# Output projection of a recurrent-memory attention kernel: partial sums per column tile, 256 columns wide, folded by a stacked identity

## The chip, the cores and the metric

The kernel runs on one core of a Trainium2 chip. A core has a matrix engine (TensorE, in the profile PE, with its weight loads as PEld), a vector engine (DVE), a scalar engine (ACT), GpSimd (POOL), and queues that start DMA transfers (here all on SP). The engines run their own instruction streams in order and wait for one another by semaphores. Matrix products are written to PSUM, eight banks of 512 float32 values in each of 128 partitions, and are read from there by ACT or DVE; PE reads its operands from SBUF. The metric is device time in microseconds of one execution, the median of the runs.

## The reference

One sequence of 2048 tokens with 512 features goes through two attentions, A and B, which a gate per token mixes. A walks through 64 segments of 32 tokens. Each segment has 8 memory rows in front, and the first 8 rows of its output are the next segment's memory: that makes the segments a chain.

```python
for s in range(n_seg):                      # 64 segments of 32 tokens
    h = jnp.concatenate([mem, xs], axis=1)  # 8 + 32 rows, 512 features
    q = jnp.einsum('btd,dhe->bhte', h, Wq)  # 32 heads of 128
    k = jnp.einsum('btd,dhe->bhte', h, Wk)
    v = jnp.einsum('btd,dhe->bhte', h, Wv)
    scores = jnp.einsum('bhqe,bhke->bhqk', q, k) * scale
    p = _softmax(jnp.where(mask, scores, -1e9))
    o = jnp.einsum('bhqk,bhke->bhqe', p, v)
    o = jnp.einsum('bhte,hed->btd', o, Wo)  # sums over 32 heads and 128 channels
    mem = o[:, :M, :]                       # the next segment's memory, M = 8
    outs.append(o[:, M:, :])
...
return g * a + (1 - g) * b                  # b: attention B, causal in 4 blocks of 512, 32 heads of 16
```

The line that the change rewrites is the product with Wo.

## The kernel before

The program is written out in full. Python code makes lists of operations for each engine (`Prog`), and `emit` turns every dependency on another engine into a semaphore wait. What stands first in an engine's list runs first.

A prologue transposes x, makes B's projections and loads the weights; it ends at a barrier some 96 us into the span. Then `plan_a` writes the 64 segments. Of the 40 rows of a segment, the 8 memory rows and the first 24 tokens make up 32 rows in `hT` (features on partitions); these are in the recurrence. The last 8 tokens of each of four segments are put together as 32 "left" rows, so their Q, K and V (`left_units`) and their product with Wo (`ol_units`) are done once per group of four. These products are fillers ("Fc") at two places in a segment: in the first three of a group six Q, K and V passes of the next group's left rows, and in the last the two halves of the former group's Wo product (`ol`).

The order within a segment is written by hand in `A_ORDER` (L823). Q0 to V1 are passes over half of the heads, 16 matmuls of 512 columns each. S, M, N are scores, softmax sums and normalisation of a half; PV is the product with V into four PSUM banks, E its copies to SBUF (`OT_sb`). W0 and W1 are the Wo product of heads 0 to 15 and 16 to 31. WT brings its result into `hT` for the next segment. The other names are fillers: bS scores a tile of B (two banks, then an exponential of 1024 columns on ACT and one or two masks on POOL), bP multiplies the oldest such tile with V, and bT does one step that waits in B's `late` list: `chain` (one small product, then three DVE steps, or seven and a sum on POOL for jobs past the first block) or `finish` (a transpose on PE, a copy on DVE, a store). bS is let through while fewer than two tiles are scored and not yet multiplied, and while the count stays on a line of 160 tiles over 57 segments. Ff makes output rows: a Wo product for B, a transpose of A's rows, the mixing.

Wo before (`out_rows`, L893): the stationary operand of a matmul is one head's 32 output rows, 128 x 32, which fills a quarter of the array's columns. Four matmuls, j = 0 to 3, take the same head four times and put a quarter of Wo's 512 columns (32-column blocks j, j+4, ...) into PSUM partitions 32j to 32j+31. All 32 heads add up in one bank of 128 columns. ACT copies it to `aW_sb` (`aO_sb` for the left rows), and a DVE transpose of 32 x 32 blocks (`flip`) turns it into `hT`'s form. POOL copies the 24 token rows to `aT_st`, where A's rows are collected for the output.

PSUM banks are handed out by `Banks`: `take` one, `pair` two neighbours, `give` back as soon as the reading operation is planned; who takes a bank next waits for that reader.

Of the kernel before, what the change touches and what calls it, by code (L numbers as in the profile page):

```python
# [223 lines left out]
def build(nc, es, A_x, A_mem0, A_Wq, A_Wk, A_Wv, A_Wo, B_wq, B_wk, B_wv, B_wo, B_beta, gate_w, out, dbg=None):  # L224
# [31 lines left out]
    def alloc(stack, *specs):  # L256
        for name, shape, dt, n in specs:
# [3 lines left out]
    alloc(es, ("ident", [128, 128], BF16, 0), ("xT", [128, C, S], BF16, 0), ("hT", [128, C, 128], BF16, 2),  # L261
# [9 lines left out]
          ("aTg", [128, C, 128], BF16, 0))  # L271
# [13 lines left out]
          ("OT_sb", [128, H, L], BF16, 0), ("OTL", [128, H, SEG], BF16, 2), ("aW_sb", [128, 128], BF16, 0), ("aO_sb", [128, 128], BF16, 0),  # L285
# [16 lines left out]
    def Rs(name):  # L302
        if name not in R:
            R[name] = Res(name)
            if name.startswith(("P0", "P1", "Pn", "R0", "R1", "OT", "aW", "aO", "t1", "aTx", "aTl")):
                R[name].readers = list(v.stores)
        return R[name]
# [60 lines left out]
def plan_const(v):  # L368
# [28 lines left out]
    def late():  # L397
        rob, rmk = Rs("onesb"), Rs("mneg")
        gp(lambda g: g.memset(onesb[:], 0.0), rob, "onesb0", True)
        gp(lambda g: g.memset(mneg[:], 0.0), rmk, "mneg0", True)  # L400
        for j in range(4):
            q = slice(32 * j, 32 * j + 32)
            gp(lambda g, q=q: g.memset(onesb[q, q], 1.0), rob, "onesb1_%d" % j)
            for i in range(4):
                o = (L + 16) * i
                sel(mneg[q, :, o + M:o + L], [[0, 4], [1, 32]], ALU.is_ge, NEG, M, -1, rmk, "mneg1_%d" % j)
                sel(mneg[q, :, o + L:o + L + 16], [[-8, 4], [0, 16]], ALU.is_ge, NEG, 0, 1, rmk, "mneg2_%d" % j)
                sel(mneg[q, :, o + L:o + L + 16], [[8, 4], [0, 16]], ALU.is_ge, NEG, 7, -1, rmk, "mneg3_%d" % j)
                sel(mneg[q, :, o + L + 8:o + L + 16], [[8, 4], [1, 8]], ALU.is_ge, NEG, 0, -1, rmk, "mneg4_%d" % j)
# [228 lines left out]
class BAttn:  # L638
# [185 lines left out]
    Q1 K0 Q0 K1 V0 TK0 TQ0 S0 bP bP TQ1 TK1 bS V1 M0 S1 N0 Fc M1 PV0 E0a N1 E0b Fc PV1 E1b E1a W0 W1 WT bS bT Ff Ff Ff  # L824
    bS bP bS""".split()
# [4 lines left out]
def plan_a(v, nseg):  # L830
# [10 lines left out]
    OT_sb, OTL, aW_sb, aO_sb, t1_sb, aT_st, g_sb, omg_sb, out2d, g_out = (  # L841
        v.OT_sb, v.OTL, v.aW_sb, v.aO_sb, v.t1_sb, v.aT_st, v.g_sb, v.omg_sb, v.out2d, v.g_out)
# [50 lines left out]
    def out_rows(bk, b, lhs, reads, name):  # L893

        def f(pe):
            ins = None
            for h in range(16 * b, 16 * (b + 1)):
                for j in range(4):
                    ins = pe.matmul(pb[bk][SEG * j:SEG * (j + 1), 0:128], lhs(h), cols(Wo_sb[:, h, :], j), start=(h == 0), stop=(h == H - 1))  # L899
            return ins  # L900
        P.op("pe", f, reads=reads + [Rs("Wo")], writes=[rbank[bk]], name=name)

    def ol_units(g):
# [5 lines left out]
        for b in range(2):  # L909
            def u(b=b):  # L910
                if b == 0:
                    st["bk"] = B.take(long=True)
                bk = st["bk"]
                out_rows(bk, b, lambda h: OTL[par][:, h, :], [Rs("OTL%d" % par)], "ol%d_%d" % (g, b))
                if b == 1:
                    evac(ENG["OL"], aO_sb[:, :], pb[bk][:, 0:128], [bk], [Rs("aO")], "olev%d" % g)
                    B.give(bk)
            units.append(("c", u))

        def ut():  # L920
            flip(aT_st[par][:, :, :].rearrange("p c (r t) -> p c r t", t=SEG)[:, :, :, SEG - 8:SEG],
                 aO_sb[:, :].rearrange("p (c r i) -> p c r i", c=C, i=8), [Rs("aO")], [Rs("aTl%d" % par)], "aTl%d" % g)
            stored.append(g)
            if g == ngrp - 1:
                return
            P.dma(P.group("as%d" % g, "as%d" % par), lambda sp: sp.dma_start(v.aTd[g], aT_st[par][:, :, :]),
                  reads=[Rs("aTl%d" % par)] + [Rs("aTx%d_%d" % (par, r)) for r in range(4)], writes=[Rs("aTd%d" % g)], name="sta%d" % g)
# [50 lines left out]
    def segment(s, fill):  # L978
# [109 lines left out]
        def wo(b):  # L1088

            if b == 0:  # L1090
                wb["bk"] = B.take()
            bk = wb["bk"]
            out_rows(bk, b, lambda h: OT_sb[:, h, 0:SEG], [Rs("OT%d_%d" % (b, half)) for half in range(2)], "wo%d_%d" % (s, b))
            if b == 1:
                evac(ENG["W"], aW_sb[:, :], pb[bk][:, 0:128], [bk], [Rs("aW")], "wev%d" % s)
                B.give(bk)

        def w_t():

            nxt = (s + 1) % 2  # L1100
            rm = Rs("hTm%d" % nxt)
            quads = hT[nxt][:, :, :].rearrange("p c (k z) -> p c k z", z=SEG)
            flip(quads[:, :, :, 0:M], aW_sb[:, :].rearrange("p (c k t) -> p c k t", c=C, t=M), [Rs("aW")], [rm], "hm%d" % (s + 1))
            P.op("gp", lambda gq: gq.tensor_copy(
                aT_st[par][:, :, SEG * r:SEG * (r + 1) - M].rearrange("p c (k t) -> p c k t", t=M), quads[:, :, 1:4, 0:M]),
                 reads=[rm], writes=[Rs("aTx%d_%d" % (par, r))], name="atx%d" % s)
# [117 lines left out]
```

The softmax here doesn't subtract the row's maximum and nothing guards it: scores larger than these inputs give would overflow.

## Time and profile before

| | |
|---|---|
| median of 3 runs | 1060.99 us (1060.31 to 1063.03) |
| span of the profiled execution | 1059.6 us |
| mean granted TensorE clock | 0.962 |
| Wo of the segments (L899, OT_sb) | 8192 matmuls, 151.8 us busy |
| Wo of the left rows (L899, OTL) | 2048 matmuls, 37.0 us busy |
| copy to aW_sb, ACT | 64 x 278 ns |
| transpose to hT, DVE | 64 x 312 ns |
| copy of rows to aT_st, POOL | 64 x 269 ns |

The profile is of one execution. In a group's line stand the line of the code, the engine, the operation, what it writes and reads, the shape and the count; then busy time, the mean duration in ns, and the engine's idle time just before these instructions with what ended it ("issue": nothing that the profile shows). A busy time is the union of the durations: four matmuls on four column tiles run side by side, so a mean duration is not a rate. In the timeline each line has the start, the duration, the engine and line, and the count of merged instructions, with the idle time before it in brackets.

### The profile page before, as it was taken

The page shows a single profiled execution, that of the slowest core. Times are in us where ns is not written, and L with a number is a line of the kernel's source. Part 1 is how long each engine was busy: PE and PEld are TensorE (multiplying, and loading weights), DVE is VectorE, ACT ScalarE, POOL GpSimd, SP SyncE. Part 2 cuts the span into 40 slices and gives each one's busy share as a digit, 9 for nine tenths or more (in the row PEclk, how much of TensorE's full clock was granted, in tenths as well). Part 3 has the DMA queues.
Part 4 walks back from the last instruction along what each step waited for, and adds up shares of the span by engine and source line. Part 5 has one row for each costly group of instructions (what it writes and reads, how often), then busy time and mean ns, then how long its engine had stood idle before and what let it go on. Part 6 is the DMA issues. An engine that isn't in the chain of part 4 may idle for free.

```text
span 1059.6 us, 65320 instructions
## 1 busy us (share of the span) xinstructions
PE 923.4 (87%) x30149; PEld 565.4 (53%) x30149; DVE 558.8 (53%) x1198; ACT 586.0 (55%) x1211; POOL 229.2 (22%) x603
## 2 busy tenths in 40 slices
PE   7967999898988989889898999899898889988886
PEld 4434555555555545555555565555555555555544
DVE  4655555453554636465465646565464546446433
ACT  4442666565665655656565656665565666544444
POOL 6100222221222122222221222222222212211010
PEclk9998999999999989999899999999899999989999
DMA  8897000000101110000001101000111001000110
GB/s 287 265 323 256 12 13 16 17 17 12 25 14 41 38 34 20 24 15 20 20 20 44 39 22 34 14 25 15 24 40 35 22 19 39 10 14 4 40 33 9
DMA packets 65929, 52.23 MB, mean 49 GB/s; under 512 B 34288, under 2 KB 64120, under 8 KB 64120
## 3 DMA queue, kind: packets, MB, share of 16 engines
q1 hardware_dynamic: 65656, 48.06, 15.5%
q8 instruction: 236, 3.87, 1.5%
q14 instruction: 37, 0.30, 0.1%
HBM read 33.47 MB, written 14.57 MB: 45 GB/s over the span
## 4 chain that ended last, share of the span: by engine, by line
PE 72%; issue 9%; ACT 8%; DVE 6%; DMA 3%; SPq 1%; ACTq 0%; POOL 0%; DVEq 0%
PE ps L862 33%; PE ps L899 17%; PE ps L706 5%; ACT PT L714 4%; PE ps L753 4%; PE ps L582 2%; DVE LN_sb L321 2%; PE ps L1061 2%; PE ps L557 2%; ACT R_sb L1043 2%; PE ps L949 2%; ACT R_sb L1040 2%; DVE Pn_sb L1047 2%; DMA scr_pQd<-stgp 1%; DMA Wo_sb<-in_A_Wo_dram 1%
## 5 line engine op out<-in xcount | busy, mean ns | idle before, releaser
L899 PE MATMUL ps<-Wo_sb,OT_sb 128*32 128x128 bf16 x8192 | 151.8, 229 | 52.5 <-issue 51.3
L714 ACT ACTIVATE PT<-ps 128x1024 bf16<-128x1024 f32 x160 | 160.5, 1023 | 26.2 <-PE ps L706 21.9
L899 PEld LDWEIGHTS ps<-Wo_sb,OT_sb 128*32 128x32 bf16 x8192 | 127.4, 101 | 67.1 <-issue 59.2
L722 POOL TENSOR_SCALAR_AFFINE_SELECT PT<-PT 128x256 bf16<-128x256 bf16 (+1 forms) x224 | 98.8, 441 | 277.0 <-ACT PT L714 269.1
L862 PE MATMUL ps<-Wq_sb,hT 128*32 128x512 bf16 x2048 | 143.9, 396 | 2.8 <-DVE hT L868 1.9
L862 PE MATMUL ps<-Wk_sb,hT 128*32 128x512 bf16 x2048 | 139.0, 387 | 0.0
L319 ACT ACTIVATE KN_sb<-ps 128x512 bf16<-128x512 f32 x128 | 76.4, 597 | 108.6 <-PE ps L862 105.8
L868 DVE STREAM_TRANSPOSE hT<-aW_sb 128x128 bf16<-128x128 bf16 x64 | 19.9, 312 | 219.9 <-ACT aW_sb L319 219.9
L862 PE MATMUL ps<-Wv_sb,hT 128*32 128x512 bf16 x2048 | 134.9, 381 | 0.8 <-ACT V_sb L319 0.8
L319 ACT ACTIVATE OT_sb<-ps 128x320 bf16<-128x320 f32 x256 | 96.9, 430 | 55.4 <-PE ps L1070 54.4
L868 DVE STREAM_TRANSPOSE KT_sb<-KN_sb 128x512 bf16<-128x512 bf16 x128 | 88.4, 690 | 48.9 <-ACT KN_sb L319 48.6
L319 ACT ACTIVATE aW_sb<-ps 128x128 bf16<-128x128 f32 x64 | 17.8, 278 | 149.3 <-PE ps L899 146.1
L868 DVE STREAM_TRANSPOSE QT_sb<-QN_sb 128x512 bf16<-128x512 bf16 x128 | 83.5, 690 | 11.7 <-ACT QN_sb L319 10.6
L1129 POOL COPY OTL<-OT_sb 128x256 bf16<-128x256 bf16 x64 | 25.5, 398 | 295.5 <-ACT OT_sb L319 295.5
L862 PEld LDWEIGHTS ps<-Wk_sb,hT 128*32 128x32 bf16 x2048 | 57.3, 99 | 59.1 <-issue 5.7
L862 PEld LDWEIGHTS ps<-Wq_sb,hT 128*32 128x32 bf16 x2048 | 51.9, 99 | 63.3 <-issue 16.6
L321 DVE CAST V_sb<-ps 128x512 bf16<-128x512 f32 x64 | 44.3, 692 | 74.9 <-PE ps L862 74.9
L862 PEld LDWEIGHTS ps<-Wv_sb,hT 128*32 128x32 bf16 x2048 | 50.4, 96 | 54.4 <-ACT P_sb L1019 9.8
L321 DVE CAST QN_sb<-ps 128x512 bf16<-128x512 f32 x64 | 44.0, 687 | 41.4 <-PE ps L862 41.3
L706 PE MATMUL ps<-QTj,KTj 32*128 32x384 bf16 (+3 forms) x512 | 64.2, 309 | 0.0
L1040 ACT ACTIVATE R_sb<-ps 128x160 f32<-128x160 f32 x128 | 38.9, 304 | 36.6 <-PE ps L1036 36.3
L1047 DVE TENSOR_TENSOR Pn_sb<-P_sb,R_sb 128x160 bf16<-128x160 bf16 x128 | 42.6, 333 | 30.9 <-ACT R_sb L1043 21.9
(117 smaller groups left out, 1424.1 us busy)
## 6 DMA issues: line engine op xcount, KB each, us to landing
Wk_sb<-in_A_Wk_dram SPq DMA_DIRECT2D x4, 1024.0 KB, 7.0
Wq_sb<-in_A_Wq_dram SPq DMA_DIRECT2D x4, 1024.0 KB, 8.6
Wv_sb<-in_A_Wv_dram SPq DMA_DIRECT2D x4, 1024.0 KB, 8.4
Wo_sb<-in_A_Wo_dram SPq DMA_DIRECT2D x4, 1024.0 KB, 10.0
scr_vd<-V SPq DMA_DIRECT2D x16, 136.0 KB, 5.3
Vj<-scr_vd SPq DMA_DIRECT2D x32, 68.0 KB, 2.4
Wo_sb<-in_A_x_dram SPq DMA_DIRECT2D x4, 512.0 KB, 7.4
scr_kTd<-stgk SPq DMA_DIRECT2D x16, 128.0 KB, 6.5
```

What stands on the lines that cost most here:

```text
L319: P.op("act", lambda a: a.activation(dst, src, ACT.Copy), reads=[v.rbank[k] for k in bks], writes=dres, name=name)
L321: P.op("dve", lambda d: d.tensor_copy(dst, src), reads=[v.rbank[k] for k in bks], writes=dres, name=name)
L706: ins = pe.matmul(v.pb[bks[x]][:, o:o + w], KT[e][r, 128 * kc:128 * (kc + 1)], QT[r, q0:q0 + w], start=True, stop=True, tile_position=(r.s ...
L714: P.op("act", lambda a: a.activation(pt[:, :, :], v.ps[:, bks[0]:bks[1] + 1, :], ACT.Exp, scale=v.SCALE_B), reads=[v.rbank[b] for b in bks ...
L722: P.op("gp", lambda g, mv=mv: g.affine_select(mv, mv, [[0, mv.shape[1]], [1, 128]], ALU.is_ge, 0.0, base=0, channel_multiplier=-1), reads= ...
L753: ins = pe.matmul(v.pb[ob][:, o:o + 17], pt[:, x, col:col + 128], V[:, kc, 17 * h:17 * (h + 1)], start=first, stop=True, skip_group_check= ...
L862: ins = pe.matmul(pb[bk][SEG * j:SEG * (j + 1), :], lhs(c), cols(w, j) if split else w[:, 512 * j:512 * (j + 1)], start=(c == 0), stop=(c ...
L868: P.op("dve", lambda d: d.transpose(dst, src), reads=reads, writes=writes, name=name)
L899: ins = pe.matmul(pb[bk][SEG * j:SEG * (j + 1), 0:128], lhs(h), cols(Wo_sb[:, h, :], j), start=(h == 0), stop=(h == H - 1))
L1040: P.op("act", lambda a: a.activation(R_sb[:, b, :], pb[bk][:, 224:384], ACT.Ln), reads=[rbank[bk]], writes=[Rs("R%d" % b)], name="ln%d_%d" ...
L1047: P.op("dve", lambda d: d.tensor_tensor(wide(Pn_sb, b)[:, :, 0:L], wide(P_sb, b)[:, :, 0:L], R_sb[:, b, :].rearrange("p (i q) -> p i q", q ...
L1129: P.op("gp", lambda gq: gq.tensor_copy(OTL[par][:, :, 8 * r:8 * r + 8], OT_sb[:, :, SEG:L]), reads=[Rs("OT%d_%d" % (c, hf)) for c in range ...
```

## The change

Four matmuls now take four different heads, 4k to 4k+3, each in its own column tile, and multiply 256 columns of Wo at once; a second set of matmuls does the other 256 columns into a second bank. After 8 steps of k, partition 32j + t of the two banks holds row t summed over the heads that are j modulo 4. These four partial sums still have to be added across partitions. `part_ev` copies each bank to bf16 on ACT (the high part) and subtracts that from the bank on DVE, which gives the rest, again in bf16 (the low part). `fold` multiplies both parts as stationary operands (128 x 128) with a stacked identity (`fold`, 128 x 32: four identities of 32 one above the other) and so adds the four partial sums and transposes the result in one go: 8 matmuls of 32 columns into one bank. DVE copies 8 columns per block of features to `hT`, ACT the other 24 to `aT_st`.

The left rows go the same way. They use `LN_sb` for the two parts, and their last unit (`ut`), a DVE transpose before, is now a fold and an ACT copy.

The order at the end of a segment changes: after W1 come bS, bT and bP, then WT, which is PE work now, then bS, Ff three times, bP and bS. `hT` is 32 columns wide instead of 128, and the stacked identity is made on POOL in the prologue.

```diff
-    Q1 K0 Q0 K1 V0 TK0 TQ0 S0 bP bP TQ1 TK1 bS V1 M0 S1 N0 Fc M1 PV0 E0a N1 E0b Fc PV1 E1b E1a W0 W1 WT bS bT Ff Ff Ff
-    bS bP bS""".split()
+    Q1 K0 Q0 K1 V0 TK0 TQ0 S0 bP bP TQ1 TK1 bS V1 M0 S1 N0 Fc M1 PV0 E0a N1 E0b Fc PV1 E1b E1a W0 W1 bS bT bP WT bS Ff Ff Ff
+    bP bS""".split()
...
+        rf = Rs("fold")
+        gp(lambda g: g.memset(v.fold[:], 0.0), rf, "fold0", True)
+        for j in range(4):
+            sel(v.fold[:], [[-1, SEG]], ALU.not_equal, 1.0, -SEG * j, 1, rf, "fold1_%d" % j)
...
-    def out_rows(bk, b, lhs, reads, name):
...
-            for h in range(16 * b, 16 * (b + 1)):
-                for j in range(4):
-                    ins = pe.matmul(pb[bk][SEG * j:SEG * (j + 1), 0:128], lhs(h), cols(Wo_sb[:, h, :], j), start=(h == 0), stop=(h == H - 1))
...
+    HD = 128 * C // 2
...
+    def out_part(bks, b, lhs, reads, name):
+
+        for hf in range(2):
+            def f(pe, hf=hf):
+                ins = None
+                for k in range(4 * b, 4 * b + 4):
+                    for j in range(4):
+                        ins = pe.matmul(pb[bks[hf]][SEG * j:SEG * (j + 1), 0:HD], lhs(4 * k + j), Wo_sb[:, 4 * k + j, HD * hf:HD * (hf + 1)],
+                                        start=(k == 0), stop=(k == 7))
+                return ins
...
+    def part_ev(bks, hi, lo, res, name):
+
+        for hf in range(2):
+            c = slice(HD * hf, HD * (hf + 1))
+            src = pb[bks[hf]][:, 0:HD]
+            P.op("act", lambda a, c=c, src=src: a.activation(hi[:, c], src, ACT.Copy), reads=[rbank[bks[hf]]],
...
+            P.op("dve", lambda d, c=c, src=src: d.tensor_tensor(lo[:, c], src, hi[:, c], ALU.subtract),
...
+    def fold(bk, hi, lo, res, name):
+
+        for hf in range(2):
+            def f(pe, hf=hf):
+                ins = None
+                for c in (2 * hf, 2 * hf + 1):
+                    for n, t in enumerate((hi, lo)):
+                        ins = pe.matmul(pb[bk][:, SEG * c:SEG * (c + 1)], t[:, 128 * c:128 * (c + 1)], v.fold[:, :], start=(n == 0), stop=(n == 1))
...
-                    st["bk"] = B.take(long=True)
...
+                    st["bks"] = B.pair()
+                out_part(st["bks"], b, lambda h: OTL[par][:, h, :], [Rs("OTL%d" % par)], "ol%d_%d" % (g, b))
                 if b == 1:
...
+                    part_ev(st["bks"], LN_sb[:, 0, :], LN_sb[:, 1, :], o_res, "olev%d" % g)
+                    B.give(*st["bks"])
...
         def w_t():
 
             nxt = (s + 1) % 2
-            rm = Rs("hTm%d" % nxt)
-            quads = hT[nxt][:, :, :].rearrange("p c (k z) -> p c k z", z=SEG)
-            flip(quads[:, :, :, 0:M], aW_sb[:, :].rearrange("p (c k t) -> p c k t", c=C, t=M), [Rs("aW")], [rm], "hm%d" % (s + 1))
-            P.op("gp", lambda gq: gq.tensor_copy(
-                aT_st[par][:, :, SEG * r:SEG * (r + 1) - M].rearrange("p c (k t) -> p c k t", t=M), quads[:, :, 1:4, 0:M]),
-                 reads=[rm], writes=[Rs("aTx%d_%d" % (par, r))], name="atx%d" % s)
+            bk = B.take()
+            src = fold(bk, v.WH, v.WL, w_res, "wf%d" % s)
+            evac("dve", hT[nxt][:, :, 0:M], src[:, :, 0:M], [bk], [Rs("hTm%d" % nxt)], "hm%d" % (s + 1))
+            evac(ENG["W"], aT_st[par][:, :, SEG * r:SEG * (r + 1) - M], src[:, :, M:SEG], [bk], [Rs("aTx%d_%d" % (par, r))], "atx%d" % s)
+            B.give(bk)
```

## The prediction

> **What bounds the kernel now.** I read the page first (busy shares, chain, groups), then the groups by form, then the timeline of single segments. One column of times runs through all: TensorE (PE) is the engine that sets the end.
>
> ```profile
> PE 923.4 (87%) x30149; PEld 565.4 (53%) x30149; DVE 558.8 (53%) x1198; ACT 586.0 (55%) x1211; POOL 229.2 (22%) x603
> ...
> PE 72%; issue 9%; ACT 8%; DVE 6%; DMA 3%; SPq 1%; ACTq 0%; POOL 0%; DVEq 0%
> ```
>
> ACT and DVE are half idle, so work added to them costs only where PE waits for it. The second line is the chain that ended last: "issue", 9%, is PE waiting for nothing visible. The groups by form say where (last columns: idle before, and what ended it):
>
> ```profile
> q8 instruction: 236, 3.87, 1.5%
> ...
> L899 PE MATMUL ps<-Wo_sb,OT_sb 128*32 128x128 bf16 x8192 | 151.8, 229 | 52.5 <-issue 51.3 <-DMA Wo_sb<-in_A_Wo_dram 1.1
> L899 PE MATMUL ps<-Wo_sb,OTL 128*32 128x128 bf16 x2048 | 37.0, 220 | 13.8 <-issue 13.8
> L1061 PE MATMUL ps<-Pn_sb,V_sb 32*128 32x40 bf16 x2048 | 36.5, 178 | 12.4 <-issue 8.4 <-DVE Pn_sb L1051 3.7
> L1070 PE MATMUL ps<-Pn_sb,VL 32*128 32x16 bf16 x2048 | 33.7, 165 | 5.7 <-issue 5.7
> ```
>
> The queue line explains it: 236 packets of 3.87 MB are 16.4 KB each, and 2 x 30149 PE instructions (a weight load and a matmul each) over 236 are 255. So PE's instructions arrive in blocks of 256. In a dense stretch the stalls sit one block apart:
>
> ```profile
> 742.56 0.52 PE L899 MATMUL ps<-Wo_sb,OTL 128*32 128x128 bf16 x24 [0.80 <-issue]
> ...
> 746.16 0.27 PE L1061 MATMUL ps<-Pn_sb,V_sb 32*128 32x40 bf16 x16 [1.68 <-issue]
> ...
> 749.91 1.04 PE L899 MATMUL ps<-Wo_sb,OT_sb 128*32 128x128 bf16 x32 [1.61 <-issue]
> ```
>
> 3.60 and 3.75 us lie between restarts with 128 matmuls (256 instructions) in each: a block is supplied in about 3.7 us, and PE stalls wherever it eats one faster. The Wo matmuls eat one in 2.
>
> The end of an undisturbed segment (start, duration), what the change rebuilds:
>
> ```profile
> 550.17 2.11 PE L899 MATMUL ps<-Wo_sb,OT_sb 128*32 128x128 bf16 x128
> ...
> 552.22 0.39 PE L706 MATMUL ps<-QTj,KTj 32*128 32x512 bf16 x2
> 552.39 0.28 ACT L319 ACTIVATE aW_sb<-ps 128x128 bf16<-128x128 f32 x1 [1.24 <-PE ps L899]
> ...
> 552.71 0.31 DVE L868 STREAM_TRANSPOSE hT<-aW_sb 128x128 bf16<-128x128 bf16 x1 [2.01 <-ACT aW_sb L319]
> 552.71 1.02 ACT L714 ACTIVATE PT<-ps 128x1024 bf16<-128x1024 f32 x1
> ...
> 553.80 0.41 POOL L722 TENSOR_SCALAR_AFFINE_SELECT PT<-PT 128x256 bf16<-128x256 bf16 x1 [0.45 <-ACT PT L714]
> ```
>
> Call T the start of the last Wo matmul (here 552.07). The carried memory is in hT at T+0.95 and the next Q pass could start at T+1.0; B's scores and PV fill that time, so the recurrence is hidden. A score tile is exponentiated (1.02) and masked (0.41) 2 us after its matmul.
>
> [...] below, 16 matmuls of 512 columns take 0.86 to 0.88 us, so 0.216 a group of four. For 256 columns I estimate 0.109 from it. [...] adot, 256 elements, 0.42 us.
>
> **The change, part by part.**
>
> *Fewer PE instructions.* Per segment 128 Wo matmuls become 64; per group of four segments the left rows' (ol) 128 become 64; each gains 8 fold matmuls. 64 x 64 + 16 x 64 - 80 x 8 = 4480 pairs less of 30149, 201 blocks for 236. Stalls now: the rows above give 51 + 14 + 8 + 6 = 79 us of issue, 82 with small rows. Idle counts from a modelled end 0.17 after the next start would have been (229 - 56 ns), so some 84 stalls hide 14 more: 96 us. After: from S1 to the end of Wo a plain segment has 72 + 32 + 16 + 64 + 32 + 64 + 128 = 408 instructions in about 5.2 us, where it had 536 in 5.3. Its densest 256 take about 2.9 us, 0.8 under the supply, the 256 before about 3.4. A stall is then 0 to 1.1 us by where the block's edge falls; I take 0.25 a segment, 16 us. Gain 80 (bounds 48, half the stalls staying, and 96).
>
> *The Wo matmuls themselves.* 16 groups of 0.109 for 32 of 0.056, but W1's first matmul waits for the last OT copy, 1.03 us after W0 began, before and after (ACT is no faster). From there 0.76 for 0.85: gain 0.09 x 64 = 6.
>
> *The chain to hT.* ACT copies of 256: between 278 (128), 430 (320) and 597 ns (512), so 0.38. First half's banks are ready 0.43 earlier. Against T: high parts end at 0.33 and 0.75, low parts (0.42 each on DVE) at 0.78 and 1.21; fold can run at 0.83 and 1.26. PE has bS and bP (0.31 + 0.25) and reaches it at about 0.8, so it waits some 0.3, then 0.14 of matmuls. The PSUM copy to hT (0.17) follows: Q possible at 1.8. Not the last wait, though.
>
> *The moved bP.* With the new order the final bP of a segment takes the tile that the bS just after W1 scored. (Before, that tile was taken in the next segment, 6 us later.) Its exp now starts after two copies, at 0.77, ends 1.79; POOL's mask is one of 0.41, two of 0.44, or one of 0.64, and the bP can start at 2.3, 2.8 or 2.5. PE is there at 1.7. Everything behind it in PE's queue, first the next Q pass, waits: Q starts at 2.6 to 3.05, mean 2.8, where it started at 1.1. One bP of 0.25 is gone from the next segment's front. Loss per plain segment 2.8 - 1.1 - 0.25, with the variants 1.38.
>
> *The chain on DVE.* bT is now ahead of the fold, so its DVE steps are ahead of the copy to hT:
>
> ```profile
> 539.86 0.22 DVE L786 RECIPROCAL rden<-ps 128x16 f32<-128x16 f32 x1
> ...
> 540.20 1.05 PE L862 MATMUL ps<-Wq_sb,hT 128*32 128x512 bf16 x16
> ...
> 541.08 1.04 PE L862 MATMUL ps<-Wk_sb,hT 128*32 128x512 bf16 x16
> ...
> 541.67 0.43 DVE L802 TENSOR_TENSOR amem<-ps,rden 128x256 f32<-128x256 f32 x1
> ...
> 541.94 1.04 PE L862 MATMUL ps<-Wq_sb,hT 128*32 128x512 bf16 x16
> ```
>
> 2.15 us from the first to the free engine. In the 24 segments with such a chain (jobs with sb above 0) hT is ready at 1.13 + 2.15 + 0.17, Q at 3.5: loss 2.1. With output rows (Ff: t1 0.87, transposes 0.22) PE is covered longer and was late before: 1.1 with a chain, 0.6 without.
>
> Counting slots by the code's rules (at most two tiles pending, 160 tiles over 57 segments): 32 x 1.38 + 14 x 2.1 + 10 x 1.1 + 2 x 0.6 = 86; the last six segments, without B tiles, lose 0.8 to 1.5: 7. Together 93 (bounds 70, if PE comes later to the bP than I count, and 110).
>
> *The left rows.* They hold a pair of banks over PV0, so PV0's second pair is now one whose Ln (L1040) must be read first: +0.47. OT's copies then queue on ACT behind the two new copies, and W0 waits for the low parts in the pair it takes over. Against shorter ol matmuls +0.5 net, in 15 segments: 7 (bounds 0 and 13). Waits that the old stalls hid (OT copies, Pn) appear: 5.
>
> *At nothing:* five GpSimd instructions for the stacked identity, where POOL has 70 us until A starts; smaller hT; the dropped POOL copy (POOL 22% busy) and its replacement on ACT, behind the exp, which nobody waits for early. No DMA is added; SP keeps its order.
>
> Sum: 93 + 7 + 5 - 80 - 6 = +19. The clean lengths that I set against stalled segments already leave out about 8 us of other waits at the segment ends (bP waiting for POOL and DMA, about 4 us in the rows; half-clock stretches), which the new wait would cover: +11. On the span, 1059.6 + 11 = 1070.6; the runs' median lies 1.4 above the span, so about 1072; I say 1071.
>
> **Rivals.** *Fetch relief wins (faster).* If almost no stall remains (gain 96) and the late bP's wait overlaps more (loss 76), 76 + 7 + 5 - 96 - 6 - 8 = -22: 1039. [...] It decides once the segment ends lose under 1.25 us on average instead of 1.45. Against it: the 2.3 to 2.8 is durations in series on three engines. *The stalls stay.* If PV and scores, still 7 ns a matmul, inherit half of them (gain 48): +43, 1104. For it: L1061 and L1070 show issue stalls now; against: these were mostly tails of runs begun by ol. *It cancels*: both large terms are within 12 us of each other, so 1058 to 1064 is no accident. *The change not doing what it says*: nothing speaks for it; the counts are fixed by the loops.
>
> **How the numbers follow.** No change is within 0.3%, about what a measurement of this kernel can tell. Forecast (1064 to 1090) 0.48; stalls stay 0.16; both slower. Fetch relief wins 0.26. Cancels 0.10. The range 1046 to 1095 takes in the cancelling case and the near halves of the outer two and leaves out a fifth; the forecast's own is 1064 to 1090.
>
> **What would show it.** PE issue idle falls from 82 to under 20; if not, the second rival. The bP matmuls (L753 before) wait for POOL's mask by some 40 us in total, Q for hT by 20 or more; if both are small, the first. Fold waits for DVE about 0.3 us each. Wo matmuls take half the count at about 275 ns. A wait of PV0 for ACT's Ln in ol segments only. It is wrong if segment ends (last Wo to Q) are under 2.2 us in the mean.

## The result, and the profile after

The changed kernel takes 1074.41 us (median of 4 runs, 1071.62 to 1077.59), the kernel before 1060.65 (4 runs beside it, 1058.26 to 1063.03). The ratio is 1.0125, with a 95% interval of 1.0081 to 1.0169: slower by a bit over one per cent. A ratio leaves out executions more than 1.5% above the fastest of the same kernel, so it can differ a little from the quotient of two medians. The profiled execution has a span of 1071.9 us, where it was 1059.6, and a mean clock of 0.968.

The page of the changed kernel, the lines that answer to those of before (busy shares, the queue that carries instructions, the chain that ended last):

```profile
PE 945.5 (88%) x25647; PEld 564.9 (53%) x25669; DVE 610.0 (57%) x1342; ACT 638.0 (60%) x1371; POOL 212.0 (20%) x544
...
q8 instruction: 202, 3.31, 1.3%
...
PE 3%; ACT 1%; DVE 1%; issue 0%; ACTq 0%
```

PE runs 4480 pairs of weight load and matmul less (the weight loads went from 30149 to 25669; the trace lacks 22 records of matmuls), and 202 instruction packets come for 236: 2 x 25669 instructions over 202 are 254 a packet, where it was 255. The chain was followed back over the last segments only (its shares add up to 5% of the span), so it can't be set against the one of before; "issue" is gone from what it shows. The groups by form say the same for the whole run (last columns: idle before, and what ended it):

```profile
L867 PE MATMUL ps<-Wq_sb,hT 128*32 128x512 bf16 x2048 | 142.3, 400 | 8.2 <-DVE hT L322 7.9
L909 PE MATMUL ps<-Wo_sb,OT_sb 128*32 128x256 bf16 x4096 | 140.6, 286 | 17.2 <-DVE LN_sb L921 9.2 <-DVE VL L322 3.0 <-DMA Wo_sb<-in_A_Wo_dram 2.3
...
L758 PE MATMUL ps<-Vj,PT 128*128 128x17 bf16 x1280 | 57.4, 172 | 26.0 <-POOL PT L727 25.3 <-issue 0.2
...
L1096 PE MATMUL ps<-Pn_sb,V_sb 32*128 32x40 bf16 x2048 | 35.9, 178 | 12.3 <-ACT R_sb L1075 6.1 <-DVE Pn_sb L1086 3.7 <-issue 1.8
...
L909 PE MATMUL ps<-Wo_sb,OTL 128*32 128x256 bf16 x1024 | 34.0, 274 | 0.2 <-issue 0.2
...
L931 PE MATMUL ps<-fold,WH 128*128 128x32 bf16 x256 | 29.2, 177 | 13.6 <-DVE WL L921 12.1
```

The Wo matmuls hardly wait for anything invisible any more (51.3 and 13.8 us before). In their place stand waits with a name: bP (L758) for POOL's mask 25.3 us, the fold (L931) for the low parts 12.1, the Q pass for hT 7.9, PV (L1096) for ACT's Ln 6.1.

Two numbers taken over all segments from the trace hold the balance. A segment's Wo matmuls, from the first start to the last, took 2.96 us in the mean and take 1.97: 63 x 0.99 = 62 us gained. From the start of the last Wo matmul to the first Q matmul of the next segment went 1.52 us in the mean and go 2.95: 63 x 1.43 = 90 us lost. The span grew by 12.3, so all the rest gained 16 by difference. One bP less at the front of 57 segments is 14 of that, by the prediction's estimate of 0.25 us each. That leaves 2 us for everything else, so what the left rows and the PV rows gained in stalls must about have been given back, to new waits such as the 9.2 us (W0 for the low parts of the left rows) and 6.1 us (Ln) in the rows above.

A segment end in the timeline (start, duration), one in which the chain of B's memory is due:

```profile
542.00 1.93 PE L909 MATMUL ps<-Wo_sb,OT_sb 128*32 128x256 bf16 x64 [0.43 <-DVE LN_sb L322]
...
543.55 0.82 ACT L919 ACTIVATE WH<-ps 128x256 bf16<-128x256 f32 x2 [1.07 <-PE ps L909]
...
543.96 0.86 DVE L921 TENSOR_TENSOR WL<-ps,WH 128x256 bf16<-128x256 f32 x2 [1.27 <-PE ps L909]
...
544.36 1.02 ACT L719 ACTIVATE PT<-ps 128x1024 bf16<-128x1024 f32 x1
...
544.74 0.25 DVE L791 RECIPROCAL rden<-ps 128x16 f32<-128x16 f32 x1
...
544.97 0.18 PE L931 MATMUL ps<-fold,WH 128*128 128x32 bf16 x1 [0.18 <-DVE WL L921]
...
545.45 0.88 POOL L727 TENSOR_SCALAR_AFFINE_SELECT PT<-PT 128x256 bf16<-128x256 bf16 x2 [2.52 <-ACT PT L719]
...
546.39 0.37 PE L758 MATMUL ps<-Vj,PT 128*128 128x17 bf16 x8 [0.84 <-POOL PT L727]
546.39 0.42 DVE L807 TENSOR_TENSOR amem<-ps,rden 128x256 f32<-128x256 f32 x1
...
546.74 0.18 DVE L322 CAST hT<-ps 128x32 bf16<-128x32 f32 x1
...
547.06 1.90 PE L867 MATMUL ps<-Wq_sb,hT 128*32 128x512 bf16 x16 [0.30 <-DVE hT L322]
```

The sum of the fold has been in PSUM since about 545.2. Its copy to hT starts only at 546.74, behind the chain on DVE (L791 to L807, 544.74 to 546.81). PE meanwhile stands at a bP, for a mask whose exponential began behind the two new copies on ACT. Two late things end close together, and the Q pass pays for the later one. The last line shows a third thing: this Q pass took 1.90 us, where one takes 1.04. The windows of the same stretch (start:end, length, busy us of PE, PEld, DVE, ACT and POOL with their counts, granted clock, DMA share, GB/s):

```profile
546.40:550.20 3.80, 3.50 (x40) 1.61 (x44) 1.21 (x3) 1.17 (x2) 2.02 (x4) 0.55 0.26 61
550.20:554.00 3.80, 3.80 (x102) 2.23 (x98) 2.61 (x4) 2.64 (x5) 0.00 (x0) 1.00 0.02 4
```

After the two waits PE works at half the clock for one window, then at the full one: the granted clock is 0.50 from 546.54 to 549.96 us and 1.00 in the 3.41 us on either side. In this profile groups of four matmuls of 512 columns in the Q, K and V passes start 0.427 us apart at half clock and 0.216 at the full one (medians), so a stretch at half clock costs at most half of its length. I had not priced that.

### The profile page after: what moved, and what is told of

It is laid out like the page before. It is cut to its first block, busy times and chain, and to the rows that moved or that the text cites. A ratio compares the mean times of both kernels' runs of the same rounds, so it can differ in the third digit from the quotient of the medians.

```text
span 1071.9 us, 56477 instructions
## 1 busy us (share of the span) xinstructions
PE 945.5 (88%) x25647; PEld 564.9 (53%) x25669; DVE 610.0 (57%) x1342; ACT 638.0 (60%) x1371; POOL 212.0 (20%) x544
## 3 DMA queue, kind: packets, MB, share of 16 engines
q8 instruction: 202, 3.31, 1.3%
## 5 line engine op out<-in xcount | busy, mean ns | idle before, releaser
L719 ACT ACTIVATE PT<-ps 128x1024 bf16<-128x1024 f32 x160 | 163.7, 1023 | 7.6 <-PE ps L711 1.8
L909 PE MATMUL ps<-Wo_sb,OT_sb 128*32 128x256 bf16 x4096 | 140.6, 286 | 17.2 <-DVE LN_sb L921 9.2
L867 PE MATMUL ps<-Wk_sb,hT 128*32 128x512 bf16 x2048 | 141.4, 398 | 0.0
L909 PEld LDWEIGHTS ps<-Wo_sb,OT_sb 128*32 128x32 bf16 x4096 | 101.7, 100 | 40.7 <-ACT OT_sb L320 12.4
L921 DVE TENSOR_TENSOR WL<-ps,WH 128x256 bf16<-128x256 f32 x128 | 54.3, 424 | 102.2 <-PE ps L909 76.6
L919 ACT ACTIVATE WH<-ps 128x256 bf16<-128x256 f32 x128 | 49.0, 383 | 69.7 <-PE ps L909 66.7
L758 PE MATMUL ps<-Vj,PT 128*128 128x17 bf16 x1280 | 57.4, 172 | 26.0 <-POOL PT L727 25.3
L758 PEld LDWEIGHTS ps<-Vj,PT 128*128 128x128 bf16 x1280 | 44.0, 96 | 41.4 <-POOL PT L727 35.9
```

What stands on the lines that cost most here:

```text
L719: P.op("act", lambda a: a.activation(pt[:, :, :], v.ps[:, bks[0]:bks[1] + 1, :], ACT.Exp, scale=v.SCALE_B), reads=[v.rbank[b] for b in bks ...
L758: ins = pe.matmul(v.pb[ob][:, o:o + 17], pt[:, x, col:col + 128], V[:, kc, 17 * h:17 * (h + 1)], start=first, stop=True, skip_group_check= ...
L867: ins = pe.matmul(pb[bk][SEG * j:SEG * (j + 1), :], lhs(c), cols(w, j) if split else w[:, 512 * j:512 * (j + 1)], start=(c == 0), stop=(c ...
L909: ins = pe.matmul(pb[bks[hf]][SEG * j:SEG * (j + 1), 0:HD], lhs(4 * k + j), Wo_sb[:, 4 * k + j, HD * hf:HD * (hf + 1)], start=(k == 0), st ...
L919: P.op("act", lambda a, c=c, src=src: a.activation(hi[:, c], src, ACT.Copy), reads=[rbank[bks[hf]]], writes=[Rs(res[0][hf])], name="%sh%d" ...
L921: P.op("dve", lambda d, c=c, src=src: d.tensor_tensor(lo[:, c], src, hi[:, c], ALU.subtract), reads=[rbank[bks[hf]], Rs(res[0][hf])], writ ...
```

## The experiments

My theory: the issue stalls are gone, as forecast, and the time went into the segment ends, half by the bP that waits for the mask, half by the chain ahead of the copy to hT. Against it stood that the gain from fewer instructions is small and the ends no worse than they must be; that one of the two waits is only in the other's shadow; and later, that the clock, not the waits, makes the difference. Medians are in us; the ratio is always to the kernel before on the same chip. The chips differ: the kernel before took 1060.65 to 1068.89 us on them, so a difference of two medians from different chips can be off by some 8 us, and the ratios decide. "Ends" is the mean from the last Wo matmul to Q; "half clock" is the time at a granted clock of one half. Both are read from one profiled execution; that of "no bP at the end" was the slowest of its 20, and by the mean clock of the others some 67 us at half clock is more usual there than 87.

| edit, on the changed kernel unless said | median | ratio, 95% interval | ends | half clock, us |
|---|---|---|---|---|
| kernel before | 1060.65 | 1 | 1.52 | 82 |
| the change | 1074.41 | 1.0125 [1.0081, 1.0169] | 2.95 | 70 |
| Wo in 128 columns | 1161.27 | 1.0950 [1.0865, 1.1036] | 2.93 | 134 |
| no bP at the end | 1059.13 | 1.0010 [0.9984, 1.0035] | 2.58 | 87 |
| chain behind the fold | 1058.26 | 0.9970 [0.9947, 0.9994] | 2.82 | 67 |
| both | 1019.82 | 0.9616 [0.9564, 0.9669] | 2.22 | 26 |
| both, Wo in 128 columns | 1120.25 | 1.0485 [1.0416, 1.0554] | 2.35 | 113 |
| kernel before, with the new order | 1164.94 | 1.0898 [1.0817, 1.0979] | 2.69 | 173 |
| the change, with the old order | 1062.61 | 0.9970 [0.9949, 0.9991] | 2.78 | 46 |
| a bP on each side of the fold | 1173.70 | 1.0978 [1.0898, 1.1058] | 3.83 | 196 |
| the same, only with two tiles | 1023.05 | 0.9630 [0.9567, 0.9693] | 2.38 | 36 |
| both, no low parts | 987.55 | 0.9244 [0.9169, 0.9319] | 1.83 | 34 |
| only with two tiles, no low parts | 991.18 | 0.9320 [0.9246, 0.9395] | 2.05 | 38 |
| the change, the wait filled | 1070.65 | 1.0042 [1.0020, 1.0064] | 3.22 | 28 |

### More instructions for the same products

Every Wo matmul of 256 columns is split into two of 128, with everything else left as it is: 5120 more pairs of weight load and matmul.

```diff
-                    for j in range(4):
-                        ins = pe.matmul(pb[bks[hf]][SEG * j:SEG * (j + 1), 0:HD], lhs(4 * k + j), Wo_sb[:, 4 * k + j, HD * hf:HD * (hf + 1)],
...
+                    for q, j in [(q, j) for q in range(2) for j in range(4)]:
+                            o = HD // 2 * q
+                            ins = pe.matmul(pb[bks[hf]][SEG * j:SEG * (j + 1), o:o + HD // 2], lhs(4 * k + j),
...
```

> The changed kernel, but each 256-column Wo matmul split into two of 128 columns in the same bank (same result, 5120 more matmul and load pairs, back to about 240 instruction blocks). Supply theory (PE eats blocks of 256 instructions faster than the 3.7 us in which one comes): PE's issue idle comes back to 40 to 80 us, the mean length of a segment's Wo run grows from 1.97 us to 2.6 or more, time 1074 + 45 to 75 = 1120 to 1150 us. Rival (the gain came from the wider columns themselves, or from the added waits giving PE nothing to stall on): two groups of 56 ns cost 3 ns more than one of 109, 16 x 80 x 3 ns = 4 us, so about 1078 us and no issue idle.

Measured: 1161.27 us, 87 more than the changed kernel, and more than expected. The groups by form of this kernel:

```profile
L910 PE MATMUL ps<-Wo_sb,OT_sb 128*32 128x128 bf16 x8192 | 153.1, 231 | 48.0 <-issue 38.7 <-DVE LN_sb L923 4.4 <-DVE VL L322 3.0
...
L910 PE MATMUL ps<-Wo_sb,OTL 128*32 128x128 bf16 x2048 | 37.5, 225 | 4.3 <-issue 4.2
```

The invisible waits are back in the Wo row, 38.7 us; over all rows of PE they are 82.1 us before, 6.8 after and 66.7 here. The instruction queue has 242 packets, where it had 202. A segment's Wo matmuls take 2.77 us instead of 1.97, 50 us in all. The part that I hadn't expected is in the table's last column: 64 us more at half clock, which cost up to 32. The same edit on the version with both waits mended (its order is shown in the next part):

> Both edits of the order, and the Wo matmuls at 128 columns as in the first run: the price of the instruction supply where segment ends give PE few waits to catch up in. Supply theory: issue idle 60 to 90 us, half clock in more than 100 us of the span, 1020 + 85 to 110 = 1105 to 1130 us. Rival (supply stalls were made by the long waits at the ends): under 1050 us.

1120.25 us for 1019.82; by the ratios (1.0485 less 0.9616) some 92 us more, and 87 us more at half clock. So the supply of instructions is worth 87 to 92 us in either order, for 5120 pairs. Of that up to 32 and 43 us are the clock, which the prediction's 80 us for 4480 pairs did not contain; without it at least 49 to 55 us remain, in the lower part of its 48 to 96.

### The two waits at the segment end

The end of the order, from W0 on, in three versions: without the last bP and bS (the tile is multiplied in the next segment); with bT behind the fold; and with both.

```diff
-W0 W1 bS bT bP WT bS Ff Ff Ff bP bS
+W0 W1 bS bT bP WT bS Ff Ff Ff
```

> The changed kernel without the last bP and bS of its order, so that this tile is multiplied in the next segment's front, as before the change. Tile theory (PE waits for the mask of a tile scored 2 us earlier): the 25 us of B's PV matmuls waiting for POOL fall under 8, segments without a long chain end (last Wo to Q) at about 1.85 us instead of 2.55 to 3.0, those with one stay at 3.4 (they wait for hT behind the chain on DVE); with 0.25 us more in the front, 34 x (-0.55) + 24 x 0.2 = -14: about 1060 us. Rival (the loss is the added work of fold, copies and low parts): 1074 us, segment ends unchanged.

```diff
-W0 W1 bS bT bP WT bS Ff Ff Ff bP bS
+W0 W1 bS bP WT bT bS Ff Ff Ff bP bS
```

> The changed kernel with bT behind WT, so that DVE copies the memory to hT before the steps of B's chain. Chain theory: segments with a long chain end at 2.5 to 3.0 (the mask) instead of 3.3 to 3.4, with output rows at 3.1; 14 x (-0.6) + 10 x (-0.25) = -11: about 1063 us; Q's wait for hT falls from 8 us to under 3. Rival (DVE's load as a whole, not its order): 1074 us.

```diff
-W0 W1 bS bT bP WT bS Ff Ff Ff bP bS
+W0 W1 bS bP WT bT bS Ff Ff Ff
```

> Both edits: bT behind WT, and the last bP and bS gone. If the two waits are all that the segment ends lost, ends fall to about 1.85 us (2.7 with output rows), 34 x (-0.55) + 14 x (-1.3) + 10 x (-0.4) = -41: about 1035 us, a little more if instruction supply stalls come back with the shorter segments (up to 1045). The added work alone (rival) would leave it at 1060 or above.

Measured: 1059.13, 1058.26 and 1019.82 us. Each alone brings 12 to 16 us, by the ratios (1.0125 less 1.0010 and less 0.9970), both together 54. The expected times were 1060, 1063 and 1035; the third was 15 us too high. The groups by form, first without the last bP, then with the chain behind the fold, then with both:

```profile
L866 PE MATMUL ps<-Wq_sb,hT 128*32 128x512 bf16 x2048 | 145.5, 407 | 28.3 <-DVE hT L322 27.6
...
L758 PE MATMUL ps<-Vj,PT 128*128 128x17 bf16 x1280 | 50.0, 171 | 0.0
```

```profile
L867 PE MATMUL ps<-Wq_sb,hT 128*32 128x512 bf16 x2048 | 140.4, 396 | 0.5 <-DVE hT L322 0.3
...
L758 PE MATMUL ps<-Vj,PT 128*128 128x17 bf16 x1280 | 57.7, 172 | 21.7 <-POOL PT L727 21.0 <-issue 0.3
```

```profile
L866 PE MATMUL ps<-Wq_sb,hT 128*32 128x512 bf16 x2048 | 134.2, 382 | 1.6 <-DVE hT L322 1.4
L758 PE MATMUL ps<-Vj,PT 128*128 128x17 bf16 x1280 | 50.3, 171 | 0.0
...
L930 PE MATMUL ps<-fold,WH 128*128 128x32 bf16 x256 | 29.0, 176 | 15.8 <-DVE WL L920 15.8
```

With the bP gone, the wait for hT rises from 7.9 to 27.6 us: most of it had been covered by the bP's. With the chain gone, the wait for the mask stays at 21.0. With both gone what is left is the fold's wait for the low parts, 15.8 us, and the time at half clock falls to 26 us. The two waits (25.3 and 7.9 us) and half of the 44 us less at half clock make 55 us, which is about what was gained. The same arithmetic is then faster than the kernel before by 3.8%. The kernel before was not run in this order, so what its own product would gain from it is not known.

### The square of products and orders

The kernel before, with its own Wo product, in the changed kernel's order:

```diff
-W0 W1 WT bS bT Ff Ff Ff bS bP bS
+W0 W1 bS bT bP WT bS Ff Ff Ff bP bS
```

> The kernel before, with nothing of the new matmuls, in the changed kernel's order. If the order is what costs (tile and chain theories), segment ends grow here too: the exp of the tile starts at 0.64 us after the last Wo matmul instead of 0.77, its mask ends at 2.1 to 2.6, and the transpose to hT stands behind B's chain (Q at 3.2): 34 x 1.05 + 14 x 1.9 + 10 x 0.9 = +71 us on 1061, with the clock halves that follow idle PE 1125 to 1155 us, while issue idle stays above 50 us. If the order is harmless and the fold's work costs, 1061 us.

1164.94 us, 10 us beyond the upper end of the expected. Two groups by form, first of the kernel before, then of this one:

```profile
L862 PE MATMUL ps<-Wq_sb,hT 128*32 128x512 bf16 x2048 | 143.9, 396 | 2.8 <-DVE hT L868 1.9 <-issue 0.6
...
L753 PE MATMUL ps<-Vj,PT 128*128 128x17 bf16 x1280 | 50.6, 171 | 5.3 <-POOL aT_st L1104 2.0 <-DMA MZj<-scr_mzd 1.7 <-issue 1.6
```

```profile
L862 PE MATMUL ps<-Wq_sb,hT 128*32 128x512 bf16 x2048 | 167.0, 456 | 3.0 <-DVE hT L868 3.0
...
L753 PE MATMUL ps<-Vj,PT 128*128 128x17 bf16 x1280 | 57.8, 172 | 56.2 <-POOL PT L722 54.7 <-issue 1.3
```

The order alone makes the bP wait 54.7 us for the mask. The Q matmuls, which follow that wait, take 456 ns in the mean where they took 396. In the profile before, 150 of these 2048 matmuls start at half clock; they take 596 ns in the mean, the others 381. The time at half clock goes from 82 to 173 us.

And the changed kernel in the old order, the reverse of that diff:

> The changed kernel with the order of the segment as it was before: W0 W1 WT bS bT Ff Ff Ff, then bS bP bS. It completes the square of the two products (one column tile, partial sums) with the two orders. Counted from the start of the last Wo matmul: with nothing in front of the fold PE waits for the low parts, fold ends at about 1.4 us, the copy to hT is not behind the chain and is done at 1.6, while PE does bS, bT, bS, bP, bS (0.9 us) and takes an old tile with bP: Q starts at about 2.3. Theory (the arithmetic gains by itself, and the loss is in the new order): mean from the last Wo matmul to Q 2.2 to 2.5 us, PE waits for the low parts about 40 us in the row of fold, for the mask under 3, time 1020 to 1040. Rival (the partial sums, with their copies and their fold, cost the segment ends as much as they save in any order, and the new order was needed for them): segment ends of 2.8 us or more and 1060 to 1080.

1062.61 us: the time is the rival's and not my theory's, and the ends of 2.78 us are all but the rival's 2.8. The mask no longer stops anybody, as my theory said. The group by form says where the time is:

```profile
L931 PE MATMUL ps<-fold,WH 128*128 128x32 bf16 x256 | 29.1, 176 | 50.1 <-DVE WL L921 49.6 <-ACT WH L919 0.4
```

With nothing between W1 and the fold, PE waits 49.6 us for the low parts (125 waits, about two in a segment); then the score tile, the product and the output rows still follow. I had counted 40 us of that wait, and had let all the rest of the end overlap. So against the kernel before the partial sums gain next to nothing in the old order (0.997), lose 1.3% in the order they came with, and gain 3.8% in one that takes bS and bP in front of the fold, which the new order rightly does, but not the bP behind it or the chain ahead of it. The rival is right for the old order and wrong with its "in any order". Set in the same new order, the partial sums are 7% faster than the old product (1.0125 for 1.0898): it is the order that loses.

### Spreading the tiles

I tried to keep a bP on each side of the fold, with one in front of the segment for two.

```diff
-W0 W1 bS bT bP WT bS Ff Ff Ff bP bS
+W0 W1 bP bS WT bP bT bS Ff Ff Ff
```

> The changed kernel with the end of a segment as W0 W1 bP bS WT bP bT bS Ff Ff Ff, and one bP only in the front: every bP takes a tile scored long before, and one bP more covers the copy to hT. Against both edits (1020 us): ends at about 1.95 us instead of 1.85, with 0.25 us less in the front, so 57 x (-0.15) = -9: about 1011 us. If something else than these two waits holds the ends, 1020 or more.

A plain miss: 1173.70 us. The group by form:

```profile
L758 PE MATMUL ps<-Vj,PT 128*128 128x17 bf16 x1280 | 57.8, 172 | 70.2 <-POOL PT L727 69.9 <-issue 0.2
```

I had assumed two tiles pending when a segment ends. There is mostly one; the first bP takes it, and the second takes the tile that was scored just before the fold: the mechanism of the change again, and stronger. With a guard that lets the second bP through only if two tiles are pending:

```diff
+        def b_q():
+            if bat.n - bat.pv_n == 2:
+                bat.pv()
...
-W0 W1 bP bS WT bP bT bS Ff Ff Ff
+W0 W1 bP bS WT bQ bT bS Ff Ff Ff
```

> The order of the spread run (W1 bP bS WT, then one bP, bT, bS), but that bP only where two tiles are pending, so that it never takes the tile scored just before WT. The spread run's 70 us of PV matmuls waiting for POOL should be gone (under 3 us), and with them the half-clock windows: one bP more than in both edits lies in the time in which hT is made, 57 x (-0.15) = -9 us against its 1020: about 1010 us. If the spread order is bad for another reason (bank reuse, ACT's queue), it stays above 1030.

1023.05 us, for 1010 expected: the wait is gone, which confirms the cause of the miss, but nothing is won over the version with both waits mended.

### Without the low parts

Each of the two orders without the low parts: the DVE subtraction and half of the fold's matmuls are left out, so the partial sums are kept as one bf16 term.

```diff
-            P.op("dve", lambda d, c=c, src=src: d.tensor_tensor(lo[:, c], src, hi[:, c], ALU.subtract),
-                 reads=[rbank[bks[hf]], Rs(res[0][hf])], writes=[Rs(res[1][hf])], name="%sl%d" % (name, hf))
...
-                    for n, t in enumerate((hi, lo)):
+                    for n, t in enumerate((hi,)):
...
```

> Both edits of the order, without the low parts: no subtraction on DVE, and the fold takes the bf16 high part alone (4 matmuls); the rounding of the partial sums to bf16 stays in the result. The two subtractions are what fold waits for (fold possible at 1.26 us, PE there at 0.85). With them gone, PE waits at the fold no longer and hT is there 0.4 us earlier: ends at 1.45 instead of 1.85, 63 x (-0.4) = -25: about 995 us. If the low part is hidden, 1015 to 1020 us.

> The same order without the low parts (no subtraction on DVE, a fold of 4 matmuls; the rounding of the partial sums stays in the result). hT is there at 1.4 us after the last Wo matmul, and PE has about 1.5 us of work until then, so no wait is left at the segment end: like both edits without low parts (988 us) or up to 9 us less, 978 to 988. If waits at the fold or for hT were all that the low part cost, the gap to the run beside it is 20 to 30 us.

987.55 and 991.18 us, the second 3 us above its expected range. In the first of them the fold's wait falls from 15.8 to 2.1 us. By the ratios the second term costs some 39 us (0.9616 less 0.9244), 14 of it that wait. What it is worth in accuracy is not shown here.

### Is it the wait, or the clock behind it?

The results beyond what I expected all had much time at half clock. To separate the standing still from the work, four matmuls that nobody reads are put before the bP that waits:

```diff
+        def idle_fill():
...
+                for c in range(4):
+                    ins = pe.matmul(pb[bk][:, 0:512], ident[:, :], Wq_sb[:, c, 0:512], start=True, stop=True)
...
-W0 W1 bS bT bP WT bS Ff Ff Ff bP bS
+W0 W1 bS bT bP WT bS Ff Ff Ff D bP bS
```

> The changed kernel with work added that nothing reads: in 57 of the 63 segments four matmuls of the identity (128x128) against 512 columns of Wq, into a free bank, issued right before the bP that waits for the mask. At the 216 ns that lie between the starts of such matmuls they are 0.86 us a segment, 49 us in all, and fall into the time in which PE stands still for the mask. Theory of the clock (a PE that stands still for about a microsecond gets half the clock for a window of 3.4 us, and the segment ends of the changed kernel pay for that besides the wait itself): time at half clock falls from 70 us to under 40, PE's wait for the mask in the row of bP from 25 us to under 8, and the time is 1055 to 1066 although work was added. Rival (the half clock follows from the mix of work or from the load, not from the standing still): time at half clock stays at 60 to 80 us, and the time is 1074 to 1085, since the added matmuls only fill a wait and overshoot it in the segments in which it is short.

The groups by form, with the added matmuls (L1159):

```profile
L758 PE MATMUL ps<-Vj,PT 128*128 128x17 bf16 x1280 | 56.9, 171 | 0.6 <-POOL PT L727 0.6
L1159 PE MATMUL ps<-Wq_sb,ident 128*128 128x512 bf16 x183 | 48.8, 379 | 6.6 <-issue 4.3 <-ACT PT L719 0.4
```

The trace has 183 of the 228 added matmuls; 48.8 us of added work, as expected. The wait for the mask is 0.6 us, the time at half clock 28 us instead of 70. The ends got longer, 3.22 us instead of 2.95, or 17 us in all. Still the kernel got no slower: 1070.65 us, where the kernel before ran at 1068.89 beside it; the ratio is 1.0042 against 1.0125 for the change. Half of the 42 us that went from half to full clock is 21, and 17 - 21 = -4; the span fell by 5.3 (1071.9 to 1066.6, on two chips), and by the ratios the fall is 9. So the rival, in which the half clock stays at 60 to 80 us, is refuted: with 48.8 us of work added in these stretches, the time at half clock fell by 42 us. The added matmuls both end the standing still and add load, so this run can't tell the one from the other. In the median itself, 1070.65 lies between the two expected ranges; by the ratio, 1.0042 x 1060.65 = 1065, it is within that of the clock theory.

No single one of these waits is as long as a window at half clock: 1.2 us was the longest of the bP's matmuls for the mask in the changed kernel, where such a window lasts 3.41 us. The last section counts the idle time ahead of each window.

## Why the prediction was right

The forecast was 1071 us, the result 1074.41. Point by point:

- *Fewer instructions, gain 80 (48 to 96).* Right in the mechanism: PE's visible issue idle was to fall from 82 to under 20 us and is 6.8. The size is less sure. The trace of before has 70 visible stalls, where the prediction counted some 84, and splitting the matmuls again costs 87 and 92 us of which up to 32 and 43 are clock. The rival in which the stalls stay is refuted.
- *The Wo matmuls, half the count at about 275 ns.* 4096 and 1024 at 286 and 274 ns. In these rows groups of four start 0.110 and 0.109 us apart (medians), for 0.109 estimated; before, with 128 columns, it was 0.056 in both.
- *The chain to hT.* Copies of 0.383 us and low parts of 0.424 us, forecast at 0.38 and 0.42. The fold waits 52 times for the low parts, 0.23 us each, forecast 0.3.
- *The moved bP, Q at 2.6 to 3.05 in plain segments.* Right: they cluster at 2.54, 2.77 and 3.02, the first a little under the range. Its wait was to show as some 40 us and shows as 25.3 on the matmuls and 35.9 on their weight loads.
- *The chain on DVE, Q at 3.5.* Right in place, slightly long: 3.31 to 3.40. But the sign by which it was to show was mis-sized. "Q for hT by 20 or more" is 7.9 us, because in those same segments PE already stands at the bP for most of the time. The run without the bP brings it out, 27.6 us. Of two waits that end close together the profile shows the second only by what is left of it; each taken away alone gave 12 and 16 us, both together 54.
- *Segment ends as a whole.* They are 2.95 us in the mean, well above the 2.2 under which the prediction was to be wrong. Forecast 93 with one bP less in the following front (57 x 0.25 = 14), so 107 at the ends themselves, less the 8 us of old waits there: 99. Measured: 90, the term that was sized 9 too long. Against it, all other terms together gained 64 us by difference (12.3 less 90, plus the 14 of the front), where they were to gain 80 + 6 - 7 - 5 = 74: the two errors cancel.
- *The left rows, PV0 waits for Ln.* 15 waits, 6.1 us (row L1096), and 9.2 us of W0 waiting for the low parts in the pair that it takes over, both foreseen; forecast 7 us net for this part.
- *The clock.* The prediction put half-clock stretches into the 8 us of "other waits" and set no price on them. That this did no harm was luck: the change took away stalls and put in waits, so that the time at half clock is 82 us before and 70 after. In the experiments, where stalls or waits grew, it counted: the expectation of the first split left it out and was 11 us too low at its upper end (1161 for at most 1150), and that of the old product in the new order put it in and was still 10 us too low (1165 for at most 1155).
- *Rivals.* Fetch relief wins was right on the supply and wrong on the ends: it needed a mean loss at the ends under 1.25 us, counted with the bP at the front and without the old waits; by that count it was (90 - 14 + 8) / 63 = 1.33, for 1.45 forecast. It is nevertheless what happens, 1019.82 us, as soon as the order is mended.

What stays open: the shares of bP and chain within the 54 us can't be given one by one, since they overlap; and the 16 us gained outside Wo and the ends were found by difference, not by an experiment. So does what the old product would do in the order that mends both waits, and whether the clock answers to waiting as such or to low load: the fill changes both. The idle time in a window was not varied by itself either; the count in the last section takes the windows as they came.

## What to carry to other kernels

Where a profile shows an engine idle for "issue" at regular distances (here 256 instructions of PE, 3.60 and 3.75 us, in the kernel before), count instructions against the supply before counting flops: splitting the Wo matmuls in two cost more here (87 us) than both mended waits brought (54). When new work goes into a dependent chain, write down for every engine what is queued ahead of each step, and move work that takes an old, finished tile to the front and work that takes the newest one away. Take away waits that end close together in one run as well as singly, because each covers the other (here 12 and 16 us singly, 54 together).

## What the hardware showed that I had not expected

The half clock comes in windows of 3.41 us or multiples of it. Of the twelve that start between 100 and 1000 us of the span, all last 3.41 us in the changed kernel; in the kernel before, eight last 3.41, three 6.83 and one 10.24. Their starts lie on a fixed grid within a run: in each of these two profiles they are whole multiples of 3.4133 us apart, to within 2 ns. None of them came behind a wholly idle window. In the changed kernel PE had been idle for 18 to 63% of the 3.41 us before each, while windows with up to 43% idle were followed by the full clock as well; in the kernel before it was 42 to 64%, and up to 49% before the full clock (matmul ends are modelled, so the shares are rough). So by this count there is no boundary.

There is one, with a narrow band between, if each matmul is counted only up to 0.17 us before its modelled end. That is the prediction's estimate of how late these ends are: 229 ns, the mean duration in the Wo row of before, less the 56 between the starts of its groups. The profiles of before and after together have 486 windows of this grid, between 117 and 1000 us, that ran at the full clock themselves. In 453 PE was idle for less than 59% by this count, and none of them was followed by half clock. In 19 it was idle for 63% or more, and every one was. Of the 14 in between, five were. As an estimate from these counts, half clock came in these two runs behind a window in which PE had less than some 1.3 to 1.4 us of work (0.37 to 0.41 of 3.41). By this count it isn't one wait that decides here but all idle time in a window. In the one ahead of the half clock of 546.54 us it is 63% by this count, and 30% by the modelled ends.

By this estimate a wait of a microsecond that returns in every segment can cost up to 1.7 us more than itself (half of 3.41) each time that it tips a window. Between the run with a bP on each side of the fold and the same with the guard the spans differ by 151 us (1171.9 less 1020.8; by the ratios 143); the wait for the mask is 70 of it, and half of the 160 us at half clock is 80.
